# Declaring a VectorE step and eight matmuls on different PSUM banks independent of each other

## The chip, the cores and the metric

The kernel runs on 1 core of one Trainium2 chip. The metric is the time of one execution on the device in microseconds (us); where runs are repeated, their median.

## The reference

Attention over keys and values that are averaged over 8 rows each, then a layer with SoLU (h times its softmax), a layer norm and a second matrix:

```
k_p, v_p = k, v averaged over 8 neighbouring rows     # q, k, v: (8, 8, 576, 64)
attn = softmax(q @ k_p.T / 8);  x = attn @ v_p         # x as (4608, 512)
h = x @ w_in                                           # (4608, 1024)
solu = h * softmax(h)
ln = (solu - mean) / sqrt(var + 1e-6) * g_ln
out = ln @ w_out                                       # (4608, 512)
```

## The kernel before, in words

The 4608 rows are 36 tiles of 128 rows. For precision, each fp32 operand of a matmul is split into an upper and a lower fp16 half, and a product is three passes: upper x upper, upper x lower, lower x upper. All that is done for a tile is cut into small operations, and the table ORDER, written out by hand, gives the order in which the operations of all tiles are issued; each engine takes its own in that order and waits, by semaphores, for what it needs of the others. The framework finds those waits by itself, from the tiles that an instruction reads and writes.

The steps of tile i that matter here:

- av (L871, TensorE) writes x, transposed, into the PSUM tile hp. hp has two banks of 512 fp32 columns each, and x takes the first 256 columns of both.
- x_hi (L879, ScalarE) rounds x to fp16 and writes the upper half of xT.
- x_lo(i, 0) and x_lo(i, 1) (L886, VectorE), called step 0 and step 1 here, form the lower half: step 0 from x's columns in hp's first bank, step 1 from those in the second.
- mm1 (L903, TensorE) multiplies by w_in and overwrites hp with h. From tile 1 on it is 24 matmuls of 128x512 in three parts: part 0 writes the first bank alone (8 matmuls: upper half of x with both halves of w_in), part 1 the second alone (8), part 2 adds the product with the lower half of x to both (8).
- h_max (L914) and the steps behind it on VectorE and ScalarE take h out of hp; av of the next tile but one overwrites it. Then come the softmax and norm, transposes by DMA (z_T, L979), and mm2 (L1036, TensorE), which multiplies by w_out.

Between av and mm1 of a tile, TensorE does the scores (L778), av and mm2 of other tiles; VectorE likewise has operations of other tiles between step 0 and step 1. In ORDER, part 0 of a tile stands behind step 0, part 1 behind step 1. Whether step 1 or part 0 is issued first differs by tile: in 14 tiles part 0 comes first (tiles 2 to 5, 7, 14, 17 to 19, 21 to 23, 32 and 33), in the other 22 step 1.

Step 0 and part 0 share the first bank, step 1 and part 1 the second. The framework looks at the tile hp, and so also has step 1 and part 0, which share none, wait for each other: whichever is issued later waits for the earlier. Tile 0 has another split of mm1 (part 0 writes both banks there).

Of the kernel before, what the change touches and what calls it, by code (L numbers as in the profile page):

```python
# [15 lines left out]
PSUM = bass.MemoryType.PSUM  # L16
# [154 lines left out]
def kernel(  # L171
# [10 lines left out]
    nc = tc.nc  # L182
# [322 lines left out]
    EARLY = 1  # L505
# [192 lines left out]
    tl = {i: {} for i in range(NT)}  # L698
# [177 lines left out]
    def x_hi(i):  # L876
# [3 lines left out]
            xT[:, 0].rearrange("p (t c) m -> p t (c m)", t=2), tl[i]["xp"], AF.Copy, scale=1.0 / S14  # L880
        )

    def x_lo(i, j):
        xT = tl[i]["xT"]
        cs = slice(2 * j, 2 * j + 2)
        nc.vector.scalar_tensor_tensor(  # L886
            out=xT[:, 1, cs].rearrange("p c m -> p (c m)"), in0=tl[i]["xp"][:, j],
            scalar=1.0 / S14, in1=xT[:, 0, cs].rearrange("p c m -> p (c m)"),
            op0=ALU.mult, op1=ALU.subtract,
        )  # L890


    def mm1(i, part):
        hp, xT = tl[i]["hp"], tl[i]["xT"]
        if i < EARLY:
            xt, wt = ((0, 0), (1, 0), (0, 1))[part]
            todo = [(f, c, xt, wt) for c in range(CI) for f in range(2)]
        elif part < 2:
            todo = [(part, c, 0, wt) for c in range(CI) for wt in range(2)]
        else:  # L900
            todo = [(f, c, 1, 0) for c in range(CI) for f in range(2)]
        for f, c, xt, wt in todo:
            nc.tensor.matmul(  # L903
                hp[:, f], lhsT=xT[:, xt, 2 * (c % 2) + c // 2],
                rhs=wi[:, wt, c, f * 512 : (f + 1) * 512],
                start=(c == 0 and xt == 0 and wt == 0), stop=(part == 2 and c == CI - 1),
            )

    def hsc(i, n):
        b, si = tile_src(i)  # L910
# [391 lines left out]
    def tile(i):  # L1302
# [35 lines left out]
        for j in range(2):  # L1338
            op("dve", 0.42, t(-1, 8.2 + 0.5 * j), x_lo, i, j, r=[("h", i)], w=[("xT1", i, j)],
               u=K("xT"), after=[n])  # L1340
        for c in range(3):
            if i < EARLY:
                ws = (
                    [("whi", "wi", d) for d in range(4)] + [("xT1", i, j) for j in range(2)], [],
                    [("wlo", "wi", d) for d in range(4)],
                )[c]
            elif c < 2:
                ws = [(nm, "wi", d) for nm in ("whi", "wlo") for d in range(4)]
                ws += [("xT1", i, c)]
            else:  # L1350
                ws = []
            prev = [op("pe", 1.727, t(0, 1.78 * c), mm1, i, c, r=K("xT") + ws, w=[("h", i)],
                       after=prev if c else ready)]
            gate.setdefault(i, prev[0])
# [107 lines left out]
```

## Time and profile before

| | |
|---|---|
| time, median of 3 runs | 494.42 us (493.95 to 495.95) |
| the profiled execution: time | 496.07 us |
| the profiled execution: span, first to last instruction | 494.3 us |
| TensorE busy (PE) | 440.6 us, 89% |
| VectorE (DVE), ScalarE (ACT), GpSimd (POOL) busy | 355.0, 351.5, 322.1 us |
| weight loads of TensorE (PEld), beside its matmuls | 213.0 us |
| DMA queue of data: share of the 16 engines' span | 80.4% |
| mm1 (L903), 864 matmuls | 199.5 us |
| mm2 (L1036), 888 matmuls | 196.5 us |
| x's lower half (L886), 72 instructions | 29.3 us |

The profile is of one execution. Busy time is the time in which an engine executes; a wait is idle time of an engine in front of an instruction, with the instruction whose end released it. The start of a matmul is recorded, its end is modelled, so rows of matmuls overlap a little. A few records of matmuls are missing, so that some rows count fewer than were run.

### The profile page before, as it was taken

To read this page: it belongs to the slowest core of one execution; us is meant where nothing else is said; L and a number is where in the kernel's file an instruction comes from. 1 tells how busy PE (TensorE), PEld (TensorE's weight loads), DVE (VectorE), ACT (ScalarE), POOL (GpSimd) and SP (SyncE) were. 2 spreads that over 40 slices of the span, in tenths; PEclk is the share of its full clock that TensorE was granted. 3 is DMA by queue.
4 is the path that set the end of the run, shared out by engine and by line. 5 is a ranking of instruction groups with operands and counts; after the bars stand their busy time and mean duration, and the time that the engine had idled before them with its cause. 6 is when DMAs were issued, how large, how long until landed. Compare 5 with 4: busy or idle time off the path is not lost.

```text
span 494.3 us, 12702 instructions
## 1 busy us (share of the span) xinstructions
PE 440.6 (89%) x4890; PEld 213.0 (43%) x4890; DVE 355.0 (72%) x879; ACT 351.5 (71%) x600; POOL 322.1 (65%) x469
## 2 busy tenths in 40 slices
PE   0076879899999899999999998999999999999996
PEld 0032334344445444544544444444544444544463
DVE  4898889839867786886877686697767768758340
ACT  3797677947976778678684597659767688557661
POOL 4272697847989667879776657867595768424440
PEclk9999799999999999999999999999999999999999
DMA  8999873994898979897899569997959696564562
GB/s 309 346 269 272 230 192 84 176 221 124 183 193 218 200 163 220 178 213 185 184 203 205 139 116 213 229 194 130 229 144 232 156 180 133 109 94 55 133 127 66
DMA packets 198460, 89.51 MB, mean 181 GB/s; under 512 B 174208, under 2 KB 182656, under 8 KB 197888
## 3 DMA queue, kind: packets, MB, share of 16 engines
q1 hardware_dynamic: 198400, 88.70, 80.4%
q8 instruction: 38, 0.62, 0.6%
q14 instruction: 22, 0.18, 0.1%
HBM read 37.75 MB, written 9.44 MB: 95 GB/s over the span
## 4 chain that ended last, share of the span: by engine, by line
PE 61%; DVE 11%; DMA 5%; ACT 3%; POOL 3%; issue 2%; SPq 1%; ACTq 0%; POOLq 0%; DVEq 0%
PE hp L903 28%; PE op L1036 27%; PE hp L871 2%; DMA eT<-e 2%; PE sc L778 2%; DVE xT L886 2%; DVE m L914 2%; DVE wo L692 1%; DVE z L949 1%; POOL z L971 1%; DMA qr<-in_q_dram 1%; DMA zT<-z 1%; DMA out_dram<-osb 1%; DVE sc L791 1%; DVE sc L802 1%
## 5 line engine op out<-in xcount | busy, mean ns | idle before, releaser
L903 PE MATMUL hp<-wi,xT 128*128 128x512 f16 x864 | 199.5, 384 | 13.0 <-DVE xT L886 12.3
L1036 PE MATMUL op<-wo,zT 128*128 128x512 f16 (+1 forms) x888 | 196.5, 374 | 2.4 <-DMA zT<-z 0.9
L903 PEld LDWEIGHTS <-xT 128*128 128x128 f16 x864 | 83.9, 98 | 116.8 <-issue 21.0
L1036 PEld LDWEIGHTS <-zT 128*128 128x128 f16 x888 | 84.3, 98 | 95.3 <-DMA zT<-z 1.6
L971 POOL TENSOR_TENSOR z<-z,z 128x512 f16<-128x512 f32 x71 | 81.8, 1163 | 36.9 <-ACT z L958 36.5
L914 DVE TENSOR_REDUCE m<-hp 128x1 f32<-128x1024 f32 x36 | 43.9, 1221 | 31.3 <-PE hp L903 31.2
L847 POOL TENSOR_TENSOR e<-e,e 128x512 f16<-128x512 f32 x36 | 41.6, 1156 | 25.2 <-ACT e L839 25.0
L342 POOL TENSOR_TENSOR vr<-vr 128x256 f32<-128x256 f32 (+2 forms) x48 | 43.1, 906 | 20.9 <-DMA vr<-in_v_dram 15.6
L963 ACT ACTIVATE z<-z,sz 128x1024 f16<-128x1024 f32 x36 | 41.2, 1145 | 19.2 <-DVE z L949 16.5
L949 DVE SCALAR_TENSOR_TENSOR z<-hp,rs,z 128x1024 f32<-128x1024 f32 x36 | 46.1, 1281 | 5.0 <-ACT z L925 3.2
L342 POOL TENSOR_TENSOR kr<-kr 128x512 f32<-128x512 f32 (+3 forms) x48 | 41.5, 869 | 11.8 <-DMA kr<-in_k_dram 10.6
L1044 ACT ACTIVATE osb<-op,f 128x512 f32<-128x512 f32 (+1 forms) x37 | 24.8, 670 | 34.0 <-issue 14.0
L886 DVE SCALAR_TENSOR_TENSOR xT<-hp,xT 128x256 f16<-128x256 f32 x72 | 29.3, 418 | 25.9 <-PE hp L903 17.1
L925 ACT ACTIVATE z<-hp,nb,Hb 128x1024 f32<-128x1024 f32 x32 | 38.3, 1198 | 13.3 <-DVE nb L917 9.9
L958 ACT ACTIVATE z<-z,sz 128x1024 f32<-128x1024 f32 x36 | 41.1, 1142 | 0.6
L984 ACT ACTIVATE junk<-z 128x1024 f16<-128x1024 f32 x36 | 37.8, 1050 | 0.4
L757 POOL TENSOR_TENSOR q<-qr,q 128x512 f16<-128x512 f32 x28 | 32.3, 1157 | 5.9 <-ACT q L747 5.3
L788 DVE TENSOR_REDUCE mx<-sc 128x8 f32<-128x576 f32 x36 | 27.1, 753 | 12.4 <-PE sc L778 12.2
L802 DVE TENSOR_REDUCE sc<-sc 128x8 f32<-128x576 f32 x36 | 27.4, 761 | 9.9 <-ACT sc L798 9.8
L879 ACT ACTIVATE xT<-hp 128x512 f16<-128x512 f32 x36 | 21.2, 588 | 12.0 <-PE hp L871 11.6
L839 ACT ACTIVATE e<-e 128x512 f16<-128x512 f32 x36 | 22.3, 618 | 9.4 <-DVE e L817 8.1
L817 DVE TENSOR_TENSOR e<-sc,r 128x576 f32<-128x576 f32 x36 | 27.2, 756 | 1.7
(229 smaller groups left out, 581.6 us busy)
## 6 DMA issues: line engine op xcount, KB each, us to landing
qr<-in_q_dram SPq DMA_DIRECT2D x16, 512.0 KB, 4.1
kr<-in_k_dram SPq DMA_DIRECT2D x16, 512.0 KB
out_dram<-osb SPq DMA_DIRECT2D x31, 256.0 KB, 2.9
wor<-in_moe_w_out_dram SPq DMA_DIRECT2D x4, 1024.0 KB
vr<-in_v_dram SPq DMA_DIRECT2D x8, 512.0 KB, 5.6
vr<-in_v_dram SPq DMA_DIRECT2D x16, 256.0 KB, 4.3
wo<-in_moe_w_in_dram SPq DMA_DIRECT2D x2, 1024.0 KB
wir<-in_moe_w_in_dram SPq DMA_DIRECT2D x2, 1024.0 KB
```

The lines of the kernel that those rows point to most:

```text
L342: nc.gpsimd.tensor_tensor(out=dst, in0=x[:, :, :n], in1=x[:, :, n : 2 * n], op=ALU.add)
L847: nc.gpsimd.tensor_tensor(out=m[:, 1], in0=em, in1=m[:, 0], op=ALU.subtract)
L886: nc.vector.scalar_tensor_tensor(out=xT[:, 1, cs].rearrange("p c m -> p (c m)"), in0=tl[i]["xp"][:, j], scalar=1.0 / S14, in1=xT[:, 0, cs] ...
L903: nc.tensor.matmul(hp[:, f], lhsT=xT[:, xt, 2 * (c % 2) + c // 2], rhs=wi[:, wt, c, f * 512 : (f + 1) * 512], start=(c == 0 and xt == 0 an ...
L914: nc.vector.tensor_reduce(out=small(i, "m"), in_=tl[i]["hp"], axis=AX.XY, op=ALU.max)
L925: nc.scalar.activation(z, t["hp"], AF.Exp, bias=t["nb"], scale=hsc(i, 0), accum_out=small(i, "se"))
L949: nc.vector.scalar_tensor_tensor(out=t["z"], in0=t["hp"], scalar=t["rs"], in1=t["z"], op0=ALU.mult, op1=ALU.mult, accum_out=small(i, "sz"),)
L958: nc.scalar.activation(t["zf"], t["zf"], AF.Identity, bias=t["sz"], scale=-float(DFF))
L963: nc.scalar.activation(t["z16"][:, 0], t["zf"], AF.Identity, bias=t["sz"], scale=-float(DFF))
L971: eng.tensor_tensor(out=t["z16"][:, 1, fs], in0=t["zf"][:, fs], in1=t["z16"][:, 0, fs], op=ALU.subtract)
L984: nc.scalar.activation(junk, t["zf"], AF.Square, scale=DFF**-0.5, accum_out=small(i, "V"))
L1036: nc.tensor.matmul(op_, lhsT=zT[:, zt, c], rhs=wo[:, wt, c, cols(hf)], start=(part == 0 and n == 0), stop=(part == 2 and n == len(todo) - 1),)
```

## The change

For every tile but tile 0, the eight matmuls of part 0 and step 1 are declared to have no dependency on each other. Where part 0 is issued after step 1, an explicit dependency of part 0's first matmul on step 0 is added. Step 0 before part 0, and step 1 before part 1, stay as they were. No operation is added, left out or moved.

```diff
--- before.py
+++ after.py
@@ -880,14 +880,33 @@
             xT[:, 0].rearrange("p (t c) m -> p t (c m)", t=2), tl[i]["xp"], AF.Copy, scale=1.0 / S14
         )
 
+    def apart(i):
+
+        t = tl[i]
+        if i < EARLY or "part0" not in t or ("lo", 1) not in t:
+            return
+        lo, late = t["lo", 1], t["last"] == "part0"
+        for mm in t["part0"]:
+            a, b = (mm, lo) if late else (lo, mm)
+            tc.declare_no_dep(a.ins, b.ins, reason="other PSUM bank")
+        if late:
+            tc.add_manual_dep(
+                t["part0"][0].ins, t["lo", 0].ins.name,
+                mybir.DependencyInfo(mybir.DependencyClass.Sync, mybir.DependencyReason.DATA),
+                reason="x's first bank is read before h is written there",
+            )
+
     def x_lo(i, j):
         xT = tl[i]["xT"]
         cs = slice(2 * j, 2 * j + 2)
-        nc.vector.scalar_tensor_tensor(
+        tl[i]["lo", j] = nc.vector.scalar_tensor_tensor(
             out=xT[:, 1, cs].rearrange("p c m -> p (c m)"), in0=tl[i]["xp"][:, j],
             scalar=1.0 / S14, in1=xT[:, 0, cs].rearrange("p c m -> p (c m)"),
             op0=ALU.mult, op1=ALU.subtract,
         )
+        if j == 1:
+            tl[i]["last"] = "lo"
+            apart(i)
 
 
     def mm1(i, part):
@@ -899,12 +918,16 @@
             todo = [(part, c, 0, wt) for c in range(CI) for wt in range(2)]
         else:
             todo = [(f, c, 1, 0) for c in range(CI) for f in range(2)]
+        did = []
         for f, c, xt, wt in todo:
-            nc.tensor.matmul(
+            did.append(nc.tensor.matmul(
                 hp[:, f], lhsT=xT[:, xt, 2 * (c % 2) + c // 2],
                 rhs=wi[:, wt, c, f * 512 : (f + 1) * 512],
                 start=(c == 0 and xt == 0 and wt == 0), stop=(part == 2 and c == CI - 1),
-            )
+            ))
+        if part == 0:
+            tl[i]["part0"], tl[i]["last"] = did, "part0"
+            apart(i)
 
     def hsc(i, n):
         b, si = tile_src(i)
```

The order of the instructions is the same on every engine; the waits that they carry differ. The rows below are the built program's order of one engine, with the semaphores that an instruction waits for in brackets (DVE_49 is VectorE's, PE_49 TensorE's, Activation_49 ScalarE's). TensorE at tile 9, part 0 and the start of part 1, before:

```order
L371 LDWEIGHTS amx_k_102 [waits DVE_49]
L371 MATMUL gk3_2602<-identb_107,amx_k_102 128x128 [waits PE_49]
L903 LDWEIGHTS xT9_2508 [waits Activation_49]
L903 MATMUL hp9_2471<-wi_88,xT9_2508 128x512 [waits DVE_49]
L903 LDWEIGHTS xT9_2508
```

and with the change (lines of the file are shifted; L923 is L903 of before), with the rows of part 0 behind it and part 1's first matmul:

```order
L371 LDWEIGHTS amx_k_102 [waits DVE_49]
L371 MATMUL gk3_2602<-identb_107,amx_k_102 128x128 [waits PE_49]
L923 LDWEIGHTS xT9_2508 [waits DVE_49]
L923 MATMUL hp9_2471<-wi_88,xT9_2508 128x512
L923 LDWEIGHTS xT9_2508
...
L923 MATMUL hp9_2471<-wi_88,xT9_2508 128x512 [waits DVE_49]
L923 LDWEIGHTS xT9_2508
```

The wait of part 0 for VectorE has moved from the first matmul to the weight load ahead of it, and part 1 has got one of its own. The rows don't show which count is waited for; in the built program part 0's is that of step 1 before and that of step 0 now, and part 1's is that of step 1. Of the 21 tiles from tile 1 on in which step 1 is issued first, part 0 waits for step 0 in 15; in tiles 8, 11, 27, 31 and 35 it still waits for step 1 (on the weight load as well), and in tile 30 it waits for neither, since TensorE has waited for a later count of VectorE before.

VectorE at tile 4, the two steps and what follows them, before:

```order
L494 CAST vbr_1_97<-vx1_1423 128x256 [waits PE_49]
L886 SCALAR_TENSOR_TENSOR xT4_1510<-hp4_1443,xT4_1510 128x256 [waits Activation_49]
L886 SCALAR_TENSOR_TENSOR xT4_1510<-hp4_1443,xT4_1510 128x256 [waits PE_49]
L788 TENSOR_REDUCE mx6_1548<-sc6_1370 128x8
L791 TENSOR_TENSOR sc6_1370<-sc6_1370,mx6_1548 128x2x288 [waits DVE_49]
```

and with the change:

```order
L494 CAST vbr_1_97<-vx1_1423 128x256 [waits PE_49]
L902 SCALAR_TENSOR_TENSOR xT4_1510<-hp4_1443,xT4_1510 128x256 [waits Activation_49]
L902 SCALAR_TENSOR_TENSOR xT4_1510<-hp4_1443,xT4_1510 128x256
L788 TENSOR_REDUCE mx6_1548<-sc6_1370 128x8
L791 TENSOR_TENSOR sc6_1370<-sc6_1370,mx6_1548 128x2x288 [waits DVE_49]
```

Step 1, the third row, no longer waits for TensorE. It is the same in all 14 tiles in which part 0 is issued first; part 0 and part 1 of those wait as before.

## Rows read from the trace of the kernel before

**Rows 1.** Stages: busy time (instructions) by engine, TensorE's granted clock, DMA share, GB/s.

```profile
core 0: us, PE busy (x) PEld busy (x) DVE busy (x) ACT busy (x) POOL busy (x), PEclk, DMA share, GB/s
45.00:105.00 60.00, 50.92 (x584) 23.46 (x578) 47.72 (x117) 45.72 (x77) 43.63 (x55) 0.94 0.80 189
105.00:470.00 365.00, 352.99 (x4005) 170.80 (x4003) 268.06 (x680) 265.30 (x452) 252.12 (x367) 1.00 0.81 171
```

**Rows 2.** Who waited for whom: us in total, times, longest us.

```profile
DVE xT L886 <- PE hp L903: 17.1, 11, 2.9
...
PE hp L903 <- DVE xT L886: 12.3, 16, 2.0
```

**Rows 3.** Timeline of tile 4: start us, us, instructions [idle before <- releaser].

```profile
103.70 0.43 DVE L886 SCALAR_TENSOR_TENSOR xT<-hp,xT 128x256 f16<-128x256 f32 x1 [2.76 <-ACT xT L879]
106.61 0.42 DVE L886 SCALAR_TENSOR_TENSOR xT<-hp,xT 128x256 f16<-128x256 f32 x1 [2.48 <-PE hp L903]
...
104.68 1.89 PE L903 MATMUL hp<-wi,xT 128*128 128x512 f16 x8
107.08 3.61 PE L903 MATMUL hp<-wi,xT 128*128 128x512 f16 x16 [0.52 <-DVE xT L886]
```

**Rows 4.** Timeline: step 1 of tiles 2, 32 and 33, part 1 of tile 17.

```profile
67.68 0.42 DVE L886 SCALAR_TENSOR_TENSOR xT<-hp,xT 128x256 f16<-128x256 f32 x1 [0.50 <-PE hp L903]
...
439.53 0.42 DVE L886 SCALAR_TENSOR_TENSOR xT<-hp,xT 128x256 f16<-128x256 f32 x1 [2.83 <-PE hp L903]
...
448.25 0.42 DVE L886 SCALAR_TENSOR_TENSOR xT<-hp,xT 128x256 f16<-128x256 f32 x1
...
255.04 3.61 PE L903 MATMUL hp<-wi,xT 128*128 128x512 f16 x16 [0.52 <-DVE pv L213]
```

**Rows 5.** Timeline of tile 9: both steps, amx_q between them, TensorE up to mm1.

```profile
160.64 0.43 DVE L886 SCALAR_TENSOR_TENSOR xT<-hp,xT 128x256 f16<-128x256 f32 x1
162.24 1.22 DVE L362 TENSOR_REDUCE amx_q<-qr 128x1 bf16<-128x1024 f32 x1 [1.18 <-DMA qr<-in_q_dram]
163.38 0.41 DVE L886 SCALAR_TENSOR_TENSOR xT<-hp,xT 128x256 f16<-128x256 f32 x1
...
162.04 0.22 PE L371 MATMUL gk<-identb,amx_k 128*128 128x128 bf16 x1
163.84 5.34 PE L903 MATMUL hp<-wi,xT 128*128 128x512 f16 x24 [1.58 <-DVE xT L886]
```

**Rows 6.** Timeline: mm1's start in tiles 1, 15, 29, 30 and 34.

```profile
58.16 3.35 PE L903 MATMUL hp<-wi,xT 128*128 128x512 f16 x8 [1.97 <-DVE xT L886]
...
229.61 5.34 PE L903 MATMUL hp<-wi,xT 128*128 128x512 f16 x24 [1.18 <-DVE xT L886]
...
397.79 2.53 PE L903 MATMUL hp<-wi,xT 128*128 128x512 f16 x11 [0.16 <-DVE pq('b', 7)_6775 L213]
...
410.96 5.34 PE L903 MATMUL hp<-wi,xT 128*128 128x512 f16 x24 [0.95 <-DVE xT L886]
...
464.42 5.34 PE L903 MATMUL hp<-wi,xT 128*128 128x512 f16 x24 [0.37 <-DVE xT L886]
```

**Rows 7.** Timeline: step 0 of tiles 1, 15 and 30.

```profile
57.23 0.41 DVE L886 SCALAR_TENSOR_TENSOR xT<-hp,xT 128x256 f16<-128x256 f32 x1
...
227.91 0.42 DVE L886 SCALAR_TENSOR_TENSOR xT<-hp,xT 128x256 f16<-128x256 f32 x1
...
406.90 0.41 DVE L886 SCALAR_TENSOR_TENSOR xT<-hp,xT 128x256 f16<-128x256 f32 x1
```

**Rows 8.** Timeline: step 1 of tile 19, and two other waits of TensorE.

```profile
282.73 0.42 DVE L886 SCALAR_TENSOR_TENSOR xT<-hp,xT 128x256 f16<-128x256 f32 x1 [2.92 <-PE hp L903]
...
286.30 0.58 PE L778 MATMUL sc<-kT,qT 64*64 64x72 f16 x48 [1.21 <-DVE pq('b', 5)_4635 L213]
...
301.01 0.36 PE L871 MATMUL hp<-eT,vb 64*64 64x128 f16 x12 [0.92 <-DMA eT<-e]
```

**Rows 9.** The chain that ended last: start us, us, what.

```profile
77.07 4.53 DVE wo L692 x4
```

**Rows 10.** The page's costliest groups: count | busy us, mean ns | idle before, releaser.

```profile
L903 PEld LDWEIGHTS <-xT 128*128 128x128 f16 x864 | 83.9, 98 | 116.8 <-issue 21.0
```

## The prediction

> **What bounds the kernel now.** I read the stages first, then who waits for whom, then the timeline around the two steps that the diff names. From 105 to 470 us TensorE is busy for 352.99 of 365.00 us, at a granted clock of 1.00, while VectorE, ScalarE and GpSimd are busy for 268, 265 and 252 [rows 1]. So TensorE sets the pace there, and all that another edit of its order can win is its idle time, 365.00 - 352.99 = 12.0 us. The list of waits says what that idle time is: TensorE's mm1 (L903) waits 16 times, 12.3 us in total, for x's lower half (L886), and in the other direction L886 waits 11 times, 17.1 us, for mm1 [rows 2]. Both are the pair that the change takes apart. The question is how much of the 12.3 us is the false wait, and whether TensorE keeps what it gets.
>
> **Part one: the second step waited for part 0 (14 tiles).** Tile 4 shows the pattern [rows 3]. Step 0 runs at 103.70 and releases part 0 at 104.68. VectorE then stands 2.48 us until part 0's last matmul has ended (the idle time in brackets at 106.61), runs step 1 for 0.42 us, and TensorE has stood 0.52 us when part 1 starts at 107.08. Step 1 reads the other bank, so without the wait it runs right behind step 0, some 2.5 us sooner, and part 1 finds it done. In 14 tiles step 1 stood behind part 0 in this way; in 11 of them part 1 follows part 0 at once on TensorE and costs it 0.52 us each, in three (3, 14 and 23) other matmuls lie between and it costs nothing. Of the 11 stalls one is in tile 2, before 105 us; ten lie after, 10 x 0.52 = **5.2 us**. The one at 255.04 is put down to another VectorE instruction, but has the same length and place [rows 4].
>
> For the stall to go, VectorE must be free at least 0.42 us and a hand-over (106.61 + 0.42 to 107.08, some 0.05 us) before part 0 ends. In ten of the 11 it had stood idle for 0.50 us or more; the least is tile 2 [rows 4]. In tile 33 step 1 (448.25) has no idle time in front of it: VectorE itself came late. I count that stall as removed all the same, because the VectorE chain ahead of it began with tile 32's step 1, which had idled 2.83 us and loses that wait [rows 4].
>
> **Part two: part 0 waited for the second step (21 tiles).** Here VectorE's order has both steps ahead of part 0, and part 0's first matmul waited for step 1. It now waits for step 0 alone in 15 tiles, and for neither in tile 30; in tiles 8, 11, 27, 31 and 35 the built program still waits for step 1, and none of these five has a stall to lose. Part 1 takes the wait for step 1 over. Tile 9 is the largest [rows 5]: TensorE is free at 162.04 + 0.22 = 162.26, step 0 has ended at 160.64 + 0.43 = 161.07, but VectorE takes amx_q in between, which waits 1.18 us for a load, so that step 1 ends at 163.79 and TensorE stands 1.58 us. Now part 0 starts at 162.26, and ends about 1.78 us later (a third of the 24 matmuls' 5.34), at 164.0; step 1 at 163.79 is 0.2 us ahead of that, so part 1 doesn't wait. Tiles 15, 30, 34 and 29 have the same with 1.18, 0.95, 0.37 and 0.16 us [rows 6]. Step 0 had ended long before in tile 30 (407.31 against 410.0) and about when TensorE came free in tile 15 (228.33 against 228.43) [rows 7]. 1.58 + 1.18 + 0.95 + 0.37 + 0.16 = **4.24 us**. Together the two parts are 9.44 of the 12.0 us.
>
> **The front.** Tile 1's stall of 1.97 us [rows 6] shrinks only by what step 1 adds behind step 0, 58.16 - (57.23 + 0.41 + 0.05) = 0.47 us [rows 6, 7], and tile 2's 0.52 us goes. But the chain of waits runs after these through VectorE's work on wo, 4.53 us without a gap at 77.07 [rows 9]. This stands behind step 1 of tile 2 in VectorE's order, so it starts sooner if its own inputs are there. Bounds 0 and 0.99 us; I take 0.5, since nothing shows which of the two waits ends last.
>
> **What comes with it.** After tile 19's step 1, which idled 2.92 us, VectorE works without a break until it releases the scores at 286.30, where TensorE stands 1.21 us [rows 8]. VectorE gets 2.92 us there and TensorE needs 0.52 + 1.21; I take the whole 1.2, with a lower bound of 0.
>
> **What it costs.** No instruction is added or moved; waits alone change. In 20 of the 21 tiles of part two the VectorE wait stands on the weight load now, not on the matmul behind it. A load takes 98 ns [rows 10]. It costs that only where TensorE arrives before step 0 is done (tiles 1 and 15, 0.2 us); at worst 20 x 0.098 = 2.0. [...]
>
> New waits are the larger unknown: a TensorE that comes sooner may find something else late. The nearest row is the eT transpose at 301.01, 0.92 us [rows 8], the only wait of TensorE for a transpose between 105 and 470 us. The bounds are none of it, and half of the 9.44; I take two such waits, 1.8 us, the value near the row, because the transposes' inputs themselves start from TensorE's results and so move with it.
>
> **Sum.** 9.44 + 0.5 + 1.2 - 0.2 - 1.8 = 9.1 us. The profiled execution took 496.07 us with a span of 494.3; it would take 487.0 with 485.2. It is 1.65 us above the median of 494.42, so the forecast for the median is 494.42 - 9.1 = **485.3 us**.
>
> **The rivals.**
> 1. *Half of it is handed on.* Each stall goes, but the next wait on TensorE takes it over. For it: SyncE's queue, VectorE and ScalarE are in-order, so one late item delays what follows. Against: in 365 us TensorE has only 12.0 - 9.44 = 2.6 us of other idle time [rows 1]. 494.42 - 4.7 = 489.7 us.
> 2. *It does nothing that counts.* TensorE's gain stays in front of something with a pace of its own. Against: no engine but TensorE is busy for more than 268 of 365 us [rows 1]. About 494 us.
> 3. *The transfers become the bound, and it gets slower.* The DMA engines are busy for 0.81 of the stretch [rows 1]; in 9.4 us less it would be 0.83. If the transposes then come as late as the one at 301.01 in every second of the 32 tiles from tile 4 on, that is 16 x 0.92 = 14.7 us, and 494.42 - 9.44 + 14.7 = 499.7 us. It decides from the eleventh such wait (11 x 0.92 = 10.1). Against: one such wait after 105 us.
> [...]
>
> **Chances.** Forecast (482.5 to 488) 0.63; rival 1 0.22; rival 2 0.08; rival 3 0.03; rival 4 0.04. What a measurement of this kernel can tell from no change is about 0.5%, 2.5 us. Faster by more than that: 0.63 + 0.22 + 0.04 = 0.89; within it 0.08; slower 0.03. The range goes down to all terms at their best (9.44 + 0.99 + 1.21, and the 0.92 at 301.01 too: 12.6 us, 481.9) and up to rival 1: 482 to 489.7 us. It leaves out rivals 2 and 3 and the outer parts of the others.
>
> **What would show it.** Right: in the list of waits mm1 behind x's lower half falls from 12.3 us to about 2.5 (tiles 0 and 1), and x's lower half behind mm1 from 17.1 us to none; TensorE's idle time in the stretch from tile 4's mm1 to tile 34's falls from 12.0 to about 4 us; step 1 follows step 0 in tile 4 within 0.1 us. Wrong: these waits are gone but waits for eT, qT or zT have grown by more than 5 us (rivals 1 and 3), or part 1 still stands behind step 1 in most of the 11 tiles.

## The result, and the profile after

| | before | with the change |
|---|---|---|
| time, median (lowest to highest) of 4 runs each | 494.57 us (493.95 to 495.95) | 480.39 us (480.17 to 480.88) |
| ratio, 95% interval | | 0.9711 [0.9689, 0.9733] |
| the profiled execution: time, span | 496.07, 494.3 us | 480.45, 478.6 us |

The change saves 14.2 us. The forecast was 9.1 us less, 485.3 us; the sign was right, the size was not: 480.4 us lies below the low end of the range (482.0). A second comparison on another chip gave the same ratio, 0.9709 [0.9665, 0.9753], though there both kernels took 2 us longer (482.41 and 496.59 us).

These lines of the changed kernel's profile page answer to the table of before (busy time by engine; TensorE's granted clock in 40 slices; the data queue; the chain of work that ended last, by engine, in which TensorE had 61% before; three groups of instructions: L923 is mm1, L902 x's lower half):

```profile
PE 434.0 (91%) x4890; PEld 211.7 (44%) x4890; DVE 356.6 (74%) x879; ACT 351.2 (73%) x600; POOL 321.9 (67%) x469
...
PEclk9999999999999999999999999999999999999999
...
q1 hardware_dynamic: 198400, 88.70, 81.7%
...
PE 75%; DVE 10%; DMA 8%; ACT 2%; issue 2%; POOL 2%; SPq 1%; ACTq 0%; POOLq 0%
...
L923 PE MATMUL hp<-wi,xT 128*128 128x512 f16 x864 | 194.7, 379 | 4.4 <-DVE xT L902 3.1
L923 PEld LDWEIGHTS <-xT 128*128 128x128 f16 x864 | 83.0, 98 | 103.7 <-issue 3.2
...
L902 DVE SCALAR_TENSOR_TENSOR xT<-hp,xT 128x256 f16<-128x256 f32 x72 | 28.9, 415 | 6.1 <-ACT xT L879 6.0
```

VectorE, ScalarE and GpSimd do the same work in nearly the same time. TensorE's busy time is 6.6 us shorter (434.0 for 440.6) although it runs the same matmuls: 4.2 us of that lie in the first 100 us, where this execution had a granted clock of 1.00 and the one before 0.97, and 2.5 us behind them, which will matter below. The list of waits shows the pair that was taken apart, in the columns of [rows 2]:

```profile
PE hp L923 <- DVE xT L902: 3.1, 3, 1.7
```

```profile
DVE m L937 <- PE hp L923: 28.9, 21, 5.1
...
DVE xT L902 <- ACT xT L879: 6.0, 7, 2.8
```

mm1's wait for x's lower half fell from 12.3 us in 16 waits to 3.1 in 3 (tiles 0, 1 and 9). The other line of [rows 2] has no counterpart: x's lower half no longer waits for mm1 at all, where it stood 17.1 us.

Where the time went is read from three stretches whose ends are the same work in both traces: the front (up to the start of tile 4's av), the middle (tile 4's av to tile 35's) and the tail. The middle and the tail of before:

```profile
102.27:461.58 359.31, 347.67 (x4014) 168.60 (x4013) 263.85 (x666) 260.31 (x445) 251.93 (x364) 1.00 0.82 174
461.58:494.30 32.72, 28.59 (x185) 15.27 (x184) 9.66 (x28) 15.39 (x23) 9.09 (x19) 1.00 0.44 99
```

and of the changed kernel (columns as in [rows 1]):

```profile
100.65:446.48 345.83, 345.34 (x4013) 168.21 (x4013) 263.55 (x666) 260.04 (x445) 251.76 (x364) 1.00 0.84 180
446.48:478.60 32.12, 28.43 (x185) 15.25 (x184) 10.19 (x28) 15.42 (x23) 9.08 (x19) 1.00 0.39 99
```

The middle is 13.48 us shorter, the tail 0.60, together 14.1 of the 14.2 us. TensorE's idle time in the middle fell from 359.31 - 347.67 = 11.64 us to 345.83 - 345.34 = 0.49 us, 11.15 us less. The other 2.33 us are busy time. Tile 4 shows what that is:

```profile
102.08 0.76 DVE L902 SCALAR_TENSOR_TENSOR xT<-hp,xT 128x256 f16<-128x256 f32 x2 [2.76 <-ACT xT L879]
...
103.05 4.26 PE L923 MATMUL hp<-wi,xT 128*128 128x512 f16 x19
```

Both steps now run back to back (x2 in one row) and part 1 follows part 0 without a gap. In [rows 3] part 1 started 107.08 - 104.68 = 2.40 us after part 0, of which the trace called 1.89 busy and 0.52 idle. Without a stall eight matmuls further on is 5.34 - 3.61 = 1.73 us (24 matmuls [rows 5] less 16 [rows 3]). So the stall cost 2.40 - 1.73 = 0.67 us: the 0.52 us shown as idle, and 0.15 us by which the last matmul ahead of a stall is shown longer, since no next one overlaps its end. The 2.33 us of busy time that went are of this kind: 17 waits of the middle went (10 stalls of part one, 4 of part two, and those at 111.50, 286.30 and 301.01, of which more below), two short ones at tile 9 and behind it came (0.22 and 0.25 us), and 2.33 / 15 = 0.155 us for each.

### The profile page after: what moved, and what is told of

It reads as the page before. It is cut to its first block, busy times and chain, and to the rows that moved or that the text cites. A ratio compares the mean times of both kernels' runs of the same rounds, so it can differ in the third digit from the quotient of the medians.

```text
span 478.6 us, 12707 instructions
## 1 busy us (share of the span) xinstructions
PE 434.0 (91%) x4890; PEld 211.7 (44%) x4890; DVE 356.6 (74%) x879; ACT 351.2 (73%) x600; POOL 321.9 (67%) x469
## 4 chain that ended last, share of the span: by engine, by line
PE 75%; DVE 10%; DMA 8%; ACT 2%; issue 2%; POOL 2%; SPq 1%; ACTq 0%; POOLq 0%
PE op L1059 34%; PE hp L923 33%; PE hp L871 3%; PE sc L778 3%; DMA qr<-in_q_dram 3%; DMA qT<-q 2%; DMA wo<-in_moe_w_in_dram 2%; DVE wo L692 2%; DMA zT<-z 1%; POOL z L994 1%; DVE wor L560 1%; DVE z L972 1%; DVE m L937 1%; DVE xT L902 1%; DVE amx_q L362 1%
## 5 line engine op out<-in xcount | busy, mean ns | idle before, releaser
L923 PE MATMUL hp<-wi,xT 128*128 128x512 f16 x864 | 194.7, 379 | 4.4 <-DVE xT L902 3.1
L923 PEld LDWEIGHTS <-xT 128*128 128x128 f16 x864 | 83.0, 98 | 103.7 <-issue 3.2
L937 DVE TENSOR_REDUCE m<-hp 128x1 f32<-128x1024 f32 x36 | 43.9, 1220 | 29.1 <-PE hp L923 28.9
L986 ACT ACTIVATE z<-z,sz 128x1024 f16<-128x1024 f32 x36 | 41.2, 1145 | 13.5 <-DVE z L972 12.5
L342 POOL TENSOR_TENSOR kr<-kr 128x512 f32<-128x512 f32 (+3 forms) x48 | 41.7, 872 | 12.3 <-DMA kr<-in_k_dram 11.1
L788 DVE TENSOR_REDUCE mx<-sc 128x8 f32<-128x576 f32 x36 | 27.1, 752 | 14.4 <-PE sc L778 14.1
L902 DVE SCALAR_TENSOR_TENSOR xT<-hp,xT 128x256 f16<-128x256 f32 x72 | 28.9, 415 | 6.1 <-ACT xT L879 6.0
```

The lines of the kernel that those rows point to most:

```text
L342: nc.gpsimd.tensor_tensor(out=dst, in0=x[:, :, :n], in1=x[:, :, n : 2 * n], op=ALU.add)
L902: tl[i]["lo", j] = nc.vector.scalar_tensor_tensor(out=xT[:, 1, cs].rearrange("p c m -> p (c m)"), in0=tl[i]["xp"][:, j], scalar=1.0 / S14, ...
L923: did.append(nc.tensor.matmul(hp[:, f], lhsT=xT[:, xt, 2 * (c % 2) + c // 2], rhs=wi[:, wt, c, f * 512 : (f + 1) * 512], start=(c == 0 and ...
L937: nc.vector.tensor_reduce(out=small(i, "m"), in_=tl[i]["hp"], axis=AX.XY, op=ALU.max)
L986: nc.scalar.activation(t["z16"][:, 0], t["zf"], AF.Identity, bias=t["sz"], scale=-float(DFF))
```

## The experiments

All runs but the last three change only which tiles `apart` takes, so that the others keep the old waits. All are timed against the kernel before on the same chip, and a gain in us is one less the ratio, times the time of that kernel.

**The two parts alone.** For tiles in which step 1 stood behind part 0 only (part one), and in which part 0 stood behind step 1 only (part two):

```diff
         lo, late = t["lo", 1], t["last"] == "part0"
+        if late:
+            return
```

This is part one alone; part two alone has `if not late` there.

> Only the 14 tiles in which part 0 is issued before step 1 are declared independent; the 21 others keep the wait of part 0 for step 1. Theory T (a stall costs its idle time plus some 0.16 us of overlap between matmuls that is lost at each restart, the VectorE time that comes free takes the waits at 286.30 and 301.01 away as well, and no new waits come): 11 x 0.67 + 1.21 + 0.92 + 0.24 = 9.7 us less than the kernel before, 9.1 if tile 2's share is lost in the front; some 485 us. Rival R (the prediction's terms: idle time alone, and new waits take some back): 5.7 + 1.2 - 1 = 5.9 us less, some 488.6 us. Rival S (the two parts stand in for each other, so that one alone gives nearly all): 12 us or more less.

> Only the 21 tiles in which step 1 is issued first are declared independent; in the 14 others step 1 still waits for part 0. T: five stalls after 105 us, 4.24 + 5 x 0.16 = 5.0 us, and 0 to 0.5 us of tile 1: 5.0 to 5.5 us less than before, some 489.3 us. R: 4.24 + 0.25 - 0.8 = 3.7 us less, some 490.9 us. S: under 3 us less, since the other part's waits take the place of these.

Part one alone: 488.27 us for 495.42, ratio 0.9844 [0.9815, 0.9872], 7.7 us less. Part two alone: 490.73 us, ratio 0.9900 [0.9878, 0.9923], 5.0 us less. The middle of the two, part one first:

```profile
103.85:453.90 350.05, 345.52 (x4012) 168.56 (x4012) 263.68 (x666) 260.45 (x445) 252.22 (x364) 1.00 0.86 179
```

```profile
101.73:456.80 355.07, 347.48 (x4014) 168.36 (x4013) 263.51 (x666) 260.12 (x445) 252.13 (x364) 1.00 0.82 176
```

Against 359.31 us that is 9.26 and 4.24 us, and 9.26 + 4.24 = 13.50 is the 13.48 of the whole change: in the middle the parts add. (That the sums agree to 0.02 us is luck, as tile 9 will show; from one tile's av to the next, the parts' gains add to the whole's within 0.11 us in every tile but 9 and 10.) Part two, with the tail's 0.52 us (32.72 - (489.0 - 456.80)), is 4.76 us, forecast at 4.24 and timed at 5.0. Part one is above the 5.2 and 1.2 us of its forecast, and above the 5.9 us of the rival (idle time alone, with some of it taken back), by its middle far above. Its time and its middle differ (7.7 us, interval 6.3 to 9.2, against 9.26): the front of the profiled execution was 1.58 us longer than before's. What the front is worth is the next experiment's question.

In part one alone, one stall is longer than before. Tile 9 in that kernel:

```profile
161.62 1.22 DVE L362 TENSOR_REDUCE amx_q<-qr 128x1 bf16<-128x1024 f32 x1 [1.85 <-DMA qr<-in_q_dram]
...
163.23 5.34 PE L925 MATMUL hp<-wi,xT 128*128 128x512 f16 x24 [2.25 <-DVE xT L904]
```

(L904 and L925 are x's lower half and mm1 in this kernel.) mm1 still stands behind step 1, which is queued behind amx_q, and amx_q waits for its load. The stall grew by 2.25 - 1.58 = 0.67 us [rows 5]. That looks like a gain given back, since everything ahead comes sooner here. But with only tile 19 changed (an experiment below), where all waits ahead of tile 19 are those of before, the stall is as long:

```profile
164.03 1.22 DVE L362 TENSOR_REDUCE amx_q<-qr 128x1 bf16<-128x1024 f32 x1 [1.85 <-DMA qr<-in_q_dram]
...
165.63 5.34 PE L923 MATMUL hp<-wi,xT 128*128 128x512 f16 x24 [2.26 <-DVE xT L902]
```

With only the front changed it is 1.25 us. So this stall differs by up to 1 us between executions in which nothing at tile 9 was changed, and the 0.67 us can't be told from chance. With both parts, the same place is:

```profile
156.13 0.42 DVE L902 SCALAR_TENSOR_TENSOR xT<-hp,xT 128x256 f16<-128x256 f32 x1 [0.15 <-ACT xT L879]
157.53 0.22 PE L371 MATMUL gk<-identb,amx_k 128*128 128x128 bf16 x1
157.59 1.89 PE L923 MATMUL hp<-wi,xT 128*128 128x512 f16 x8
158.09 1.22 DVE L362 TENSOR_REDUCE amx_q<-qr 128x1 bf16<-128x1024 f32 x1 [1.54 <-DMA qr<-in_q_dram]
159.23 0.41 DVE L902 SCALAR_TENSOR_TENSOR xT<-hp,xT 128x256 f16<-128x256 f32 x1
...
159.70 3.61 PE L923 MATMUL hp<-wi,xT 128*128 128x512 f16 x16 [0.22 <-DVE xT L902]
```

Part 0's 1.89 us now cover the wait for the load, all but 0.22 us: the mechanism that the forecast described, with step 1 0.2 us late in this execution instead of 0.2 us early.

**The front and the middle alone.** Tiles 1 to 3 only, and tiles 4 to 35 only:

```diff
-        if i < EARLY or "part0" not in t or ("lo", 1) not in t:
+        if i < EARLY or i > 3 or "part0" not in t or ("lo", 1) not in t:
```

```diff
-        if i < EARLY or "part0" not in t or ("lo", 1) not in t:
+        if i < 4 or "part0" not in t or ("lo", 1) not in t:
```

> The change in tiles 1 to 3 alone. T: the front's part of the gain, 1.0 us (tile 1 0.47, tile 2 0.52 + 0.16) to the 1.6 us by which the changed kernel is ahead at av of tile 4 in its trace. R: 0 to 0.5 us, the wo work on VectorE hides it. The clock as a cause: a gain that comes and goes with the granted clock of the run (0.993 or 1.00).

> The change in tiles 4 to 35 alone. T: 14.2 us less 1.0 to 1.6 us of the front, so 12.6 to 13.2 us less than before, some 481.7 us. R: 8 us less.

The front alone: 495.59 us, ratio 0.9997 [0.9972, 1.0021], nothing that can be measured. The middle alone: 482.24 us, ratio 0.9728 [0.9702, 0.9753], 13.5 us less. My theory for the front (1.0 to 1.6 us) had come from the profiled executions alone, in which the front is 102.27 us before and 100.65 after. The stretch from 0 to tile 4's av in four executions, first the two of the kernel before and with only the front changed:

```profile
0.00:102.27 102.27, 64.39 (x695) 29.14 (x695) 81.44 (x185) 75.79 (x132) 61.03 (x88) 0.97 0.88 232
```

```profile
0.00:103.13 103.13, 64.96 (x695) 29.42 (x695) 82.93 (x185) 75.74 (x132) 61.45 (x88) 0.95 0.89 230
```

and two executions of the changed kernel:

```profile
0.00:100.65 100.65, 60.19 (x696) 28.22 (x697) 82.82 (x185) 75.73 (x132) 61.07 (x88) 1.00 0.92 239
```

```profile
0.00:101.79 101.79, 64.24 (x695) 29.40 (x695) 83.19 (x185) 75.90 (x132) 61.15 (x88) 0.97 0.90 236
```

At the same granted clock of 0.97 the changed kernel's front is 0.48 us shorter than before's, and the longest and the shortest of the four, at 0.95 and 1.00, lie 2.48 us apart. But the clock doesn't sort the fronts either. At 0.95 both of these were seen, first with the front unchanged (tiles 4 to 35 only), then with part one:

```profile
0.00:101.68 101.68, 66.00 (x695) 29.64 (x695) 82.37 (x185) 75.85 (x132) 60.59 (x88) 0.95 0.87 233
```

```profile
0.00:103.85 103.85, 64.66 (x695) 29.48 (x695) 82.76 (x185) 75.66 (x132) 60.69 (x88) 0.95 0.88 229
```

So the front differs between executions by more than the change could give there, for causes that stay open, and one profile can't price it. My 1.0 to 1.6 us fell: the timed runs put it at 0.1 us (-1.0 to 1.4). Why so little is left shows in the timeline. Tile 2's stall of 0.52 us is gone in the changed kernel, but all of its mm1 now starts behind a new wait for VectorE (the instruction named follows step 0 at once):

```profile
64.11 5.34 PE L923 MATMUL hp<-wi,xT 128*128 128x512 f16 x24 [1.32 <-DVE pq('b', 1)_759 L389]
```

A wait of 1.16 to 1.59 us stands there in all seven traces in which TensorE comes sooner (tile 1 changed, or two matmuls fewer, as in the last experiment but one), and in none of the four others. In the two traces of the changed kernel the later wait for VectorE's wo grew too, from 0.76 us to 1.34 and 1.33. So in the front another wait for VectorE takes over, as rival 1 had it for the whole; that it takes just what was won isn't shown.

**Tile 19.** Behind its stall of 0.52 us, two other waits of TensorE follow, 1.21 and 0.92 us [rows 8], which the changed kernel doesn't have:

```profile
271.33 0.75 DVE L902 SCALAR_TENSOR_TENSOR xT<-hp,xT 128x256 f16<-128x256 f32 x2
...
272.87 3.62 PE L923 MATMUL hp<-wi,xT 128*128 128x512 f16 x16
...
276.42 0.58 PE L778 MATMUL sc<-kT,qT 64*64 64x72 f16 x48
...
290.04 0.34 PE L871 MATMUL hp<-eT,vb 64*64 64x128 f16 x12
```

Is that this one tile's doing? Only tile 19 changed, and all but tile 19:

```diff
-        if i < EARLY or "part0" not in t or ("lo", 1) not in t:
+        if i != 19 or "part0" not in t or ("lo", 1) not in t:
```

```diff
-        if i < EARLY or "part0" not in t or ("lo", 1) not in t:
+        if i < EARLY or i == 19 or "part0" not in t or ("lo", 1) not in t:
```

> The kernel before with the change in tile 19 alone, whose step 1 idled 2.92 us. T (the VectorE time that this wait held back is what TensorE waited for at 286.30 and, through the eT transpose, at 301.01): from av of tile 19 to av of tile 22 TensorE needs 0.67 + 1.25 + 1.12 = 3.0 us less than before (before: 38.33 us), and the kernel is some 3 us faster. Rival (those waits have other causes, and went in part_one because other tiles' waits went): 0.5 to 0.7 us less.

> The change in all tiles but 19. T: the waits of 0.52, 1.21 and about 0.9 us (mm1, scores, av) are back in their places and no others are; av of tile 19 to av of tile 22 takes as long as before, some 38.3 us, the kernel 483.4 us. Rival: TensorE waits 0.52 us once more, 481.1 us.

Only tile 19: 493.51 us for 495.22, ratio 0.9951 [0.9924, 0.9978], 2.4 us less. From tile 19's av to tile 22's, first before, then with only tile 19 changed:

```profile
276.35:314.68 38.33, 35.17 (x395) 16.96 (x393) 26.75 (x71) 27.62 (x47) 26.69 (x37) 1.00 0.85 166
```

```profile
278.16:313.54 35.38, 34.86 (x395) 16.94 (x393) 26.83 (x71) 27.74 (x47) 26.18 (x37) 1.00 0.90 177
```

The change in one tile shortens its surroundings by 2.95 us, over four times what its own stall cost (0.67 us). With all but tile 19 changed (484.13 us, ratio 0.9751 [0.9715, 0.9788], some 2 us less of a gain than the whole change) both waits are back, in sizes like those of before (1.21 and 0.92):

```profile
280.58 0.58 PE L778 MATMUL sc<-kT,qT 64*64 64x72 f16 x48 [1.21 <-DVE pq('b', 5)_4635 L213]
...
295.13 0.36 PE L871 MATMUL hp<-eT,vb 64*64 64x128 f16 x12 [0.75 <-DMA eT<-e]
```

The expectation was missed in two points. From tile 19's av to tile 22's this kernel takes 308.13 - 270.63 = 37.50 us and not 38.3, since tile 21, whose stall lies in that stretch, is changed too. And a wait of 0.56 us for a zT transpose at 325.01 came, where the changed kernel has none. The two waits themselves went with tile 19's change alone and came back without it. So they hang on the 2.92 us that VectorE lost in front of tile 19's step 1 [rows 8]: it was late for the scores by one chain and, through them, for the softmax whose transpose eT is.

**How much room do the other engines have?** If TensorE's gain is kept because the other engines have slack, then TensorE could be freed of more work and keep that too. Two matmuls less per tile in part 2 (their product is left out of the result), once in the changed kernel and once in the kernel before:

```diff
-            todo = [(f, c, 1, 0) for c in range(CI) for f in range(2)]
+            todo = [(f, c, 1, 0) for c in range(CI - 1) for f in range(2)]
...
-                start=(c == 0 and xt == 0 and wt == 0), stop=(part == 2 and c == CI - 1),
+                start=(c == 0 and xt == 0 and wt == 0), stop=(part == 2 and c == (CI - 1 if i < EARLY else CI - 2)),
```

> The changed kernel with 22 instead of 24 matmuls of mm1 in each of the tiles 1 to 35: the product of x's lower half with the last of the four row blocks of w_in is left out. That is 35 x 2 x 0.216 = 15.1 us less of TensorE's time. T (after tile 4 TensorE alone sets the pace, everything else starts from its results and moves with it): 12 us or more less than the changed kernel, 468 us or less, and under 3 us of idle time of TensorE from av of tile 4 to av of tile 35. Rival (the other engines or the transposes were only just hidden): under 8 us less, and 6 us or more of new waits of TensorE.

> The kernel before, in which part 2 of mm1 leaves out the product of x's lower half with the last row block of w_in (two matmuls of 128x512 less in each of 35 tiles, 35 x 2 x 0.216 = 15.1 us of TensorE's work), so that its output is not the reference's. All false waits are as before. It tells whether TensorE alone can take what it is freed of, or whether the change could keep all of its gain only because VectorE was freed as well. Theory (VectorE's freedom matters): here TensorE alone gets ahead and VectorE still stands behind part 0 in 11 tiles, so that half or more is handed on: 7 us or less below the kernel before, with 6 us or more of TensorE's idle time in the middle above that of before, in waits for VectorE and the transposes. Rival (the other engines have room as long as TensorE's stalls remain): 11 us or more below the kernel before, since it has 11.6 us of idle time in which the others already run ahead.

With the change: 475.2 us, ratio to the kernel before 0.9585 [0.9546, 0.9624], against 0.9711 for the change alone: some 6 us less for 15.1 us of work. Without it: 488.2 us, ratio 0.9827 [0.978, 0.9873], 8.6 us less, between the two expectations. The theory of the first run (12 us or more) falls, and so does the rival of the second (11 us or more). The theory of the second isn't met either: it asked for 6 us more of TensorE's idle time in the middle, and 352.22 - 336.66 = 15.56 us is 3.9 more. The middle of the first, and what TensorE waits for there:

```profile
102.10:441.92 339.82, 333.58 (x3950) 161.72 (x3949) 262.92 (x666) 260.20 (x445) 251.57 (x364) 1.00 0.87 183
```

```profile
PE gq('b', 5)_4589 L371 <- DVE amx_q L362: 1.8, 1, 1.8
PE op L1059 <- DMA zT<-z: 1.2, 3, 0.7
PE gk L371 <- DVE amx_k L362: 0.7, 1, 0.7
PE sc L778 <- ACT z L981: 0.6, 1, 0.6
```

and of the second:

```profile
102.61:454.83 352.22, 336.66 (x3950) 163.02 (x3949) 263.80 (x666) 260.53 (x445) 252.06 (x364) 1.00 0.84 177
```

```profile
PE hp L903 <- DVE xT L886: 8.4, 14, 1.2
PE gk L371 <- DVE amx_k L362: 2.1, 1, 2.1
PE sc L778 <- DVE pq('b', 5)_4599 L213: 1.2, 1, 1.2
PE hp L871 <- DMA eT<-e: 0.9, 2, 0.7
```

The four kernels make a square (middle, us; the work removed in it is 31 x 2 x 0.216 = 13.4 us):

| | all of mm1 | two matmuls fewer | gained by less work |
|---|---|---|---|
| waits as before | 359.31 | 352.22 | 7.09 |
| false waits gone | 345.83 | 339.82 | 6.01 |
| gained by the change | 13.48 | 12.40 | |

Less work is handed on by half in both rows: in the first, waits for VectorE's amx_q (behind a load) and amx_k (behind GpSimd), for transposes and for ScalarE take its place, so the other engines have little room. The change is kept in both columns, 12.40 us even where TensorE is already early. So general slack isn't why it was kept. Nor does the false wait on VectorE explain why less work is handed on in the kernel before, as I had expected there: the changed kernel, without it, hands on as much.

What tells stalls from work may be how far VectorE falls behind. Its wait for mm1's end, ahead of h_max, is its reserve; before, in the kernel before with less work, and in the changed kernel with less work it is

```profile
DVE m L914 <- PE hp L903: 31.2, 22, 4.9
```

```profile
DVE m L914 <- PE hp L903: 21.3, 15, 4.1
```

```profile
DVE m L937 <- PE hp L923: 20.0, 15, 4.1
```

and 28.9 us with the change alone. Less work takes 9 to 10 us of the reserve; the change takes 2.3, and it gives VectorE the 17.1 us that it had stood in front of step 1. The two parts fit this: with part one alone, which frees VectorE, the wait is 32.9 us, more than before, and with part two alone, which frees only TensorE, 27.5. But that this is the cause is argued from these rows, not shown: part two was kept as well, though it is only 4.8 us, and a kernel that removes as many stalls of TensorE without freeing VectorE wasn't tried.

**The changed kernel again**, on the chip of the last run:

> The changed kernel once more, on the same chip as the run beside it. If the gain of 14 us and the clock at 1.00 throughout were a matter of one chip, it would come out 9 to 11 us below the kernel before with waits like those forecast; otherwise at a ratio of 0.969 to 0.973, with TensorE's idle time in the middle of 0.5 us again.

482.41 us, ratio 0.9709 [0.9665, 0.9753]. TensorE's idle time in the middle is 346.21 - 345.55 = 0.66 us:

```profile
101.79:448.00 346.21, 345.55 (x4012) 168.11 (x4011) 263.60 (x666) 260.62 (x445) 252.03 (x364) 1.00 0.87 180
```

## Why the prediction was right and wrong

What bounds the kernel was right: TensorE's idle time was the prize, the false waits were nearly all of it, and behind the front no other engine took the gain. Rivals 1 to 3 fell with it: no new wait above 0.25 us stands in the middle (0.29 in the second trace of this kernel, 0.43 with only tiles 4 to 35 changed), and the DMA share rose from 0.82 to 0.84 without one. What rival 1 said of the queues the traces show: SyncE, VectorE and ScalarE run their work in the same order in the traces of both kernels, and step 1 of tile 9 stands behind amx_q and its wait of 1.18 us [rows 5]. But behind the front nothing that came late took the gain. Rival 4, a rise of the granted clock from its 0.94 between 45 and 105 us [rows 1], isn't where the gain came from: the middle, where the gain lies, had a clock of 1.00 before and has it now, the second comparison has the same ratio with a clock of 0.97 in the front, and with only the front's stalls removed the front's clock was 0.95.

Term by term, the measured sizes from the starts of av, tile by tile, in the two traces:

| term of the sum | forecast | measured |
|---|---|---|
| part one: ten stalls after 105 us | 5.2 | 10 x 0.67 = 6.7 |
| part two: five stalls | 4.24 | 0.95 (tile 9) + 1.22 (15) + 0.32 (29) + 1.00 (30) + 0.60 (tail, with 34) = 4.1 |
| the front | 0.5 | 0.1 (-1.0 to 1.4) |
| what comes with it | 1.2 | 3.3 (13.48 less the above: 6.7 and 3.49) |
| weight-load waits | -0.2 | 0 |
| new waits | -1.8 | 0 (the 0.22 and 0.25 us at tile 9 and behind it are in its 0.95; those of the front in its 0.1) |
| sum | 9.1 | 14.2 |

The 0.95 of tile 9 holds the chance of that execution's load (1.24 with tile 10 in the second trace).

Of the 5.1 us between the sums, three steps make 5.4 (2.1 + 1.8 + 1.5); the weight loads add 0.2, and the front and part two take back 0.5.

1. **"What comes with it" was looked for at one place only, 2.1 us short.** VectorE got back 17.1 us, and I priced that where I had followed it, at 286.30. The wait for eT at 301.01 (1.11 us gained there) hung on the same 2.92 us, as the runs with tile 19 show. Tile 5 gained 1.50 us where its own stall is worth 0.67; there a wait of 0.24 us for VectorE's e at 111.50, which I hadn't counted, is gone too, worth 0.4 us with its lost overlap; the other 0.4 us are delays of some 0.1 us, too short for a bracket, with their overlap:

```profile
111.50 0.58 PE L778 MATMUL sc<-kT,qT 64*64 64x72 f16 x48 [0.24 <-DVE e L817]
```

2. **"New waits are the larger unknown" took the sign from the wrong row, 1.8 us.** I took the wait at 301.01 as a sample of what TensorE would meet if it came sooner. It was a consequence of the false wait and went with it, as the runs with tile 19 show. Behind the front no wait above 0.25 us took its place.
3. **The stalls were sized by the bracket, 1.5 us.** The idle time in the profile, 0.52 us, is what is left after the last matmul's modelled end. The distance between the starts, less that of an unstalled group, is 0.67 us. With this size for the ten stalls of part one the low end of the range would have been 480.4 us.

The weight-load wait cost nothing that the trace shows: 20 weight loads now carry a wait for VectorE, TensorE is idle for 0.49 us in 345.83, and in tiles 12, 16, 24, 25 and 28, whose waits moved and which had no stall, the time from av to the next tile's av is that of before within 0.02 us. The upper bound of 2.0 us is excluded. That a load costs its 98 ns only where TensorE comes before step 0 has ended was my estimate; no run shows that cost.

Tile 33, whose stall I removed because VectorE's lateness began with tile 32, behaved so: it gained 0.68 us like the others. (The chain runs through ScalarE: VectorE's z, delayed by tile 32's step 1, held ScalarE for 1.98 us at 441.71, and ScalarE's x_hi of tile 33 then held VectorE for 1.71 us at 445.74.)

## What to carry to other kernels

A framework that tracks dependencies by tile makes false waits where two engines use different banks of one tile; look in the list of waits for a pair that waits in both directions (12.3 and 17.1 us here), since removing it can free both engines (the 17.1 us of VectorE's waits went, and 11.15 us of TensorE's idle time in the middle), and count every wait behind the second engine's lost time as part of the gain. Price a stall of TensorE by the distance of the starts around it (0.67 us here), not by the idle time in its bracket (0.52 us). Before you charge a forecast with new waits, see whether the row that they are priced by is itself a consequence of what the change removes, as the 0.92 us at 301.01 was.

## What the hardware showed that was not expected

- A stall of 0.52 us between matmuls of 128x512 cost 0.67 us, and 0.15 us of that stands in the trace as busy time.
- The first 100 us vary by some 3.2 us between the eleven traces (100.65 to 103.85), and by 2.2 us at one granted clock (0.95), while the middle of one kernel repeated within 0.4 us (345.83 and 346.21).
